# The start of a fused attention and maxout kernel: first query pair in two halves, last key piece in two loads, no later dummy matmuls, new order of the first 400 steps

## The chip, the core and the metric

One core of a Trainium2 chip runs the whole kernel. The metric is the device time of one execution in microseconds, the median of the runs shown. A profile is one execution taken by the hardware profiler; times in it count from the span's start.

## What is computed

Four batches of 12288 queries attend to 768 keys each, and the result goes through a maxout network. Keys and values are the same array: kv averaged over 4 x 4 blocks and multiplied by `w_sr`.

```python
kv_pool = kv.reshape(B, H // r, r, W // r, r, C).mean(axis=(2, 4))     # r = 4, C = 128
k = v = kv_pool.reshape(B, -1, C) @ w_sr                               # 768 x 128 per batch
a = softmax(scale * (q @ k.T)); x = (a @ v).reshape(-1, 128)           # 49152 x 128
h = max(x @ w1, x @ w2, x @ w3)                                        # 49152 x 768
out = h @ w_out
```

The weights of the network are 64-bit floats. All products are done in float16 with each operand split into a high and a low part, so that a product of two matrices is three matmuls (high by high, high by low, low by high).

## The kernel before

The 49152 queries are 96 groups of 512 (`g`); a group is four tiles of 128 (`j`). Two neighbouring groups share one load of q, a pair of 512 KB.

The work is cut into steps, each named by a short token, and the order of all steps is written out by hand in tables of tokens: `START` (the prologue and the first groups), `STEADY` (repeated 41 times) and `END`. Every engine executes its instructions in the order of the table. A token with `!` runs the step on VectorE, with `%` on GpSimd, instead of its usual engine. The tokens that matter here:

- `kv.s.i`, `wd.n.h`, `qd`: loads of a kv piece (12 of 512 KB), of half a weight matrix (8 of 384 KB) and of q. All are issued by SyncE (SP) into one queue, as are the transposing DMAs.
- `add`, `gat`, `end`: kv pieces are added in place, then transposed and summed by fp32 matmuls with the identity (gather). `gathered` copies the result out of PSUM, `gathered_peak` takes its maximum, `gathered_project` multiplies it by `w_sr`, `gathered_hi` and `gathered_lo` split it into the keys' two parts `k_hi`, `k_lo`; `value` transposes these by DMA into `v_hi`, `v_lo`.
- `qc`, `qp`, `qu`, `qh`, `ql`, `qt`, `qe`: a group of q is multiplied by a column scale, its row maximum is taken over the pair (`q_peak`; with `!` a sum of absolute values on ScalarE), a power of two is made of it, the high and the low part are formed and transposed by DMA into `qT`.
- `S`: the scores of one tile, six matmuls into `ps_s` (two buffers). `m`: their row maximum `mx` and the bias `nb` (VectorE); `e`: exponential (ScalarE); `c`: its high part `ahl` (ScalarE, or VectorE with `!`); `l`: its low part (GpSimd); `lt`: a transposing DMA into `aT`.
- `X`: attention weights by values, for group 0 tile by tile, later in two halves per group; `xh`, `xl` split the result.
- `H`: six matmuls for one 128-column slice of the hidden layer into two buffers `ps_h`; `R`, `M`: relu and maximum of the two; `C`, `L`: high and low part; `O`: three matmuls with `w_out`, six for a group's last slice.
- `wm`, `ws`, `wl`: a 64-bit weight piece becomes fp32 (ScalarE scales, VectorE shifts and adds the low bits into `w_three`); `wr` subtracts the first matrix from the others, `wh` and `wo` split into `d_hi`, `d_lo`. `dsize`, `turn_w1`, `product`, `usize` are the few matmuls of the weights' own sizing and product.
- `warm.n`: n dummy matmuls of 256 columns with the identity into `ps_o`; nothing reads them (`keep_warm`, line 349).

In the kernel before, `START` has four `warm.8` before the first `S` and 12 `warm.4` and one `warm.8` up to the first `H`, 88 dummies in all. The profile shows all instructions at line 105, the wrapper that keeps program order, so tiles identify them.

Of the kernel before, what the change touches and what calls it, by code (L numbers as in the profile page):

```python
# [9 lines left out]
F32 = mybir.dt.float32  # L10
F16 = mybir.dt.float16
# [10 lines left out]
def kernel(  # L22
# [34 lines left out]
    R = 4  # L57
# [67 lines left out]
    def times(t, src, by, by2=None):  # L125
# [261 lines left out]
    class Keys:  # L387
# [18 lines left out]
        def load(self, s, i):  # L406
            piece = kvp.tile([P, PIECE], F32, name="kv_piece")
            src = kv[self.b].rearrange("(s h i) (w r) c -> s i h w (r c)", s=KS, i=R, w=KW)
            sp_dma.dma_start(out=piece, in_=src[s, i])
            self.pieces[s, i] = piece  # L410
# [177 lines left out]
    def q_load(s):  # L588
        t = qp.tile([P, SJ, C], F32, name="q_sb", bufs=2)
        sp_dma.dma_start(out=t, in_=q_src[s])  # L590
        st["q"][s] = t
# [8 lines left out]
    def q_peak(s, summed=False):  # L600

        assert not {2 * s, 2 * s + 1} & set(todo["qc"])
        row = qp.tile([P, 1], F32, name="q_row", bufs=2)
        if summed:
            act.activation(
                out=qp.tile([P, 3 * HALF_F], F16, name="q_abs", bufs=1)[:, :SJ * C], in_=st["q"][s].rearrange("p j c -> p (j c)"),
                func=AF.Abs, accum_out=row,
            )
        else:
            dve.tensor_reduce(out=row, in_=st["q"][s], axis=AX.XY, op=ALU.max, apply_absolute_value=True)  # L610
        st["qr"][s] = row

    def q_up(s):
        row = st["qr"][s]
        up = qp.tile([P, 1], F32, name="q_up", bufs=2)
        dve.tensor_scalar(
            out=row.bitcast(I32), in0=row.bitcast(I32), scalar1=EXPO, scalar2=None, op0=ALU.bitwise_and
        )
        dve.tensor_scalar(out=up, in0=row, scalar1=TINY, scalar2=2.0 ** -14, op0=ALU.max, op1=ALU.mult)
        dve.reciprocal(out=up, in_=up)  # L620
        st["qr"][s] = (row, up)

    def q_hi(g, on=None):
        hl = qp.tile([P, NJ, 2, C], F16, name="q_hl", bufs=2)
        if on:
            on.tensor_scalar(
                out=hl[:, :, 0], in0=q_half(g), scalar1=st["qr"][g // 2][1], scalar2=None, op0=ALU.mult
            )
        else:
            act.mul(out=hl[:, :, 0], in_=q_half(g), mul=st["qr"][g // 2][1])  # L630
        st["qhl"][g] = hl

    def q_lo(g):
        t, hl = q_half(g), st["qhl"][g]
        up = st["qr"][g // 2][1]
# [12 lines left out]
    def q_exps(s):  # L648
        sc = qp.tile([P, 1], F32, name="q_sc", bufs=4)
        dve.tensor_scalar(  # L650
            out=sc, in0=st["qr"][s][0], scalar1=TINY, scalar2=KT[2 * s // GPB].g_exp, op0=ALU.max, op1=ALU.mult
# [25 lines left out]
    def soft_bias(g, j, negated):  # L677
        nb = tiny.tile([P, 1], F32, name="nb")
        dve.tensor_scalar(
            out=nb, in0=negated, scalar1=st["sc"][g // 2], scalar2=LN_A_UP, op0=ALU.mult, op1=ALU.add  # L680
# [489 lines left out]
```

## Time and profile before

| | before |
|---|---|
| median of 3 runs | 1973.16 us (1973.13 to 1973.49) |
| span of the profiled execution | 1971.1 us, 29575 instructions |
| TensorE busy | 1961.7 us (100%) |
| VectorE busy | 1473.6 us (75%) |
| ScalarE busy | 1486.3 us (75%) |
| GpSimd busy | 1271.3 us (64%) |
| DMA | 284.61 MB, mean 144 GB/s |

The profile gives no device time of the profiled execution other than its span, from the first to the last instruction; the runs' median lies 2.1 us above it. Busy shares are means over the run. Matmuls are pipelined and their ends are modelled, so a busy TensorE says that matmuls followed each other, not that they were useful: the dummies count too. Idle time of another engine costs nothing as long as TensorE has work.

### The profile page before, as it was taken

The numbers are of one execution on the slowest core, as the hardware profiler recorded it, in microseconds if no ns is written. First come the engines' busy times: TensorE is split into PE (matmuls) and PEld (weight loads), VectorE is DVE, ScalarE is ACT, GpSimd is POOL, SyncE is SP. The second block draws the span as 40 slices with busy tenths as digits, with TensorE's granted clock in tenths as the row PEclk, the third lists the DMA queues.
The fourth block names the chain that finished last, engine by engine and source line by source line (L and its number), as shares of the span: only waits on it lengthen the run. The fifth ranks groups of instructions, "written<-read, shape, count | busy, mean of one in ns | idle before, by whom it ended". The sixth has DMA issues, their size and how long they took to land.

```text
span 1971.1 us, 29575 instructions
## 1 busy us (share of the span) xinstructions
PE 1961.7 (100%) x9869; PEld 964.2 (49%) x9869; DVE 1473.6 (75%) x2558; ACT 1486.3 (75%) x2620; POOL 1271.3 (64%) x934
## 2 busy tenths in 40 slices
PE   8999999999999999999999999999999999999999
PEld 7444444444444444444444444444444444444444
DVE  7998987777767787777667777777766676767677
ACT  5866677787777777777777777777777777777775
POOL 3644566666676666766666676666676666666663
PEclk9999999999999999999999999999999999999999
DMA  9977577767678767767678767866776666756763
GB/s 285 179 166 147 111 161 138 148 132 138 129 152 162 158 145 159 147 126 137 138 133 164 156 147 157 164 128 129 137 145 136 129 126 128 144 123 127 134 128 81
DMA packets 845241, 284.61 MB, mean 144 GB/s; under 512 B 818720, under 2 KB 819872, under 8 KB 845088
## 3 DMA queue, kind: packets, MB, share of 16 engines
q1 hardware_dynamic: 844800, 282.58, 70.5%
q8 instruction: 78, 1.28, 0.3%
q14 instruction: 75, 0.61, 0.1%
q10 hardware_dynamic: 288, 0.13, 0.0%
HBM read 53.54 MB, written 25.17 MB: 40 GB/s over the span
## 4 chain that ended last, share of the span: by engine, by line
PE 98%; DMA 1%; DVE 0%; ACT 0%; SPq 0%; issue 0%; DVEq 0%; ACTq 0%
PE ps_h L105 38%; PE ps_o L105 22%; PE ps_x L105 19%; PE ps_s L105 19%; DMA kv_piece<-in_kv_dram 0%; DMA aT<-ahl 0%; SPq L105 0%; ACT a L105 0%; DVE q_row L105 0%; DVE kv_piece L105 0%; DVE k_lo L105 0%; ACT w_three L105 0%; DVE mx L105 0%; ACT ahl L105 0%; ACT k_hi L105 0%
## 5 line engine op out<-in xcount | busy, mean ns | idle before, releaser
L105 POOL TENSOR_TENSOR hl<-h,hh 128x512 f16<-128x512 f32 x461 | 551.5, 1202 | 513.8 <-ACT hh L105 512.0
L105 POOL TENSOR_TENSOR ahl<-a,ahl 128x768 f16<-128x768 f32 (+1 forms) x378 | 618.2, 1655 | 136.3 <-ACT ahl L105 103.3
L105 DVE SCALAR_TENSOR_TENSOR h<-ps_h,h 128x512 f32<-128x512 f32 x574 | 395.5, 689 | 344.5 <-PE ps_h L105 190.2
L105 ACT ACTIVATE h<-ps_h 128x512 f32<-128x512 f32 x574 | 342.3, 596 | 284.1 <-PE ps_h L105 274.0
L105 PE MATMUL ps_h<-xh,d_hi 128*128 128x512 f16 x1148 | 435.1, 379 | 0.0
L105 PE MATMUL ps_h<-xh,d_lo 128*128 128x512 f16 x1148 | 435.1, 379 | 0.0
L105 PE MATMUL ps_h<-xl,d_hi 128*128 128x512 f16 x1148 | 435.1, 379 | 0.0
L105 DVE TENSOR_REDUCE mx<-ps_s 128x1 f32<-128x768 f32 x384 | 365.1, 951 | 50.3 <-PE ps_s L105 50.2
L105 ACT ACTIVATE a<-ps_s,nb,q_sc 128x768 f32<-128x768 f32 x384 | 379.6, 989 | 14.1 <-DVE nb L105 13.4
L105 PE MATMUL ps_s<-k_hi,qT 128*128 128x384 f16 x1536 | 374.6, 326 | 0.0
L105 ACT CAST hh<-h 128x512 f16<-128x512 f32 x577 | 336.6, 613 | 42.6 <-DVE h L105 41.4
L105 PE MATMUL ps_x<-aT,v_hi 128*128 128x512 f16 (+1 forms) x1188 | 367.2, 373 | 0.2 <-DMA aT<-ahl 0.2
L105 PEld LDWEIGHTS <-d_hi 128*128 128x128 f16 x2308 | 225.8, 98 | 256.6
L105 PE MATMUL ps_o<-hh,wo 128*128 128x512 f16 x1140 | 339.1, 379 | 0.0
L105 PEld LDWEIGHTS <-qT 128*128 128x128 f16 x2304 | 225.4, 98 | 187.4
L105 ACT CAST ahl<-a 128x768 f16<-128x768 f32 x367 | 300.1, 829 | 5.3
L105 PEld LDWEIGHTS <-wo 128*128 128x128 f16 x1710 | 167.3, 98 | 191.7
L105 PE MATMUL ps_s<-k_lo,qT 128*128 128x384 f16 x768 | 250.2, 326 | 0.0
L105 PE MATMUL ps_x<-aT,v_lo 128*128 128x512 f16 (+1 forms) x594 | 220.2, 373 | 0.0
L105 PE MATMUL ps_o<-hl,wo 128*128 128x512 f16 x570 | 216.0, 379 | 0.0
L105 PEld LDWEIGHTS <-v_hi 128*128 128x128 f16 x1188 | 115.3, 98 | 134.7 <-issue 0.5
L105 PEld LDWEIGHTS <-d_lo 128*128 128x128 f16 x1154 | 112.9, 98 | 120.9
(151 smaller groups left out, 1459.1 us busy)
## 6 DMA issues: line engine op xcount, KB each, us to landing
kv_piece<-in_kv_dram SPq DMA_DIRECT2D x48, 512.0 KB, 4.5
q_sb<-in_q_dram SPq DMA_DIRECT2D x48, 512.0 KB, 4.4
out_dram<-o_sb SPq DMA_DIRECT2D x95, 256.0 KB, 2.0
aT<-ahl SPq DMA_TRANSPOSE x384, 4.0
kv_piece<-in_moe_w_dram SPq DMA_DIRECT2D x6, 384.0 KB, 9.4
qT<-q_hl SPq DMA_TRANSPOSE x96, 3.6
o_turned<-o_planes SPq DMA_TRANSPOSE x95, 3.4
kv_piece<-in_moe_w_out_dram SPq DMA_DIRECT2D x2, 384.0 KB, 7.7
```

The lines of the kernel that those rows point to most:

```text
L105: return lambda **kw: tc.keep_in_program_order(op(**kw))
```

## The change

1. The first q pair is loaded in two halves, one group each: `unit` and `unit_q` map the step numbers, so that `qd`, `qp`, `qu` and `qe` exist once for group 0, once for group 1 and then once for each pair (49 in place of 48). The first half is loaded first of all, the second behind two kv pieces.
2. The last kv piece (`kv.0.2`) is loaded in two halves of 256 KB.
3. All dummies after the first score tile are gone (12 `warm.4` and the `warm.8` after the first scores), and two batches between gather and scores. Three `warm.8` remain, one at the very start.
4. `START` has a new order up to step 399 (408 before). From there on the tables are word for word the same, and up to there both have issued the same work. In these steps some work has moved between engines: two of the kv additions (`add.1.0.1%`, `add.0.2.3.0%`) to GpSimd; two subtractions `wr` and two products `qc` from VectorE to GpSimd; seven casts `c`, four high parts `qh`, one `wh` and one `gathered` from ScalarE to VectorE; the first maximum of q partly to ScalarE.

```diff
@@ the table, two of its rows around the first H
-        "dsize.1 product dsized.1 ratio S m c X wo.1.0 l e X usize l xh warm.4 c l m usized xl produced qe S e H R",
+        "dsized.1 ka ratio lt c X m usize wo.1.0 e qt S qe usized lt xh wo.2.0 qd S xl produced c l m H R e M H R lt m",
...
-        def load(self, s, i):
-            piece = kvp.tile([P, PIECE], F32, name="kv_piece")
-            src = kv[self.b].rearrange("(s h i) (w r) c -> s i h w (r c)", s=KS, i=R, w=KW)
-            sp_dma.dma_start(out=piece, in_=src[s, i])
-            self.pieces[s, i] = piece
+        def load(self, s, i, *us):
+
+            if (s, i) not in self.pieces:
+                self.pieces[s, i] = kvp.tile([P, PIECE], F32, name="kv_piece")
+            piece = self.pieces[s, i]
+            src = kv[self.b].rearrange("(s h i) (w r) c -> s i h w (r c)", s=KS, i=R, w=KW)[s, i]
+            if us:
+                x = slice(us[0] * PIECE // KU, (us[0] + 1) * PIECE // KU)
+                piece, src = piece[:, x], src[:, :, x]
+            sp_dma.dma_start(out=piece, in_=src)
...
-    def q_load(s):
-        t = qp.tile([P, SJ, C], F32, name="q_sb", bufs=2)
-        sp_dma.dma_start(out=t, in_=q_src[s])
-        st["q"][s] = t
+    def unit(g):
+
+        return g if g < 2 else g // 2 + 1
+
+    def unit_q(u):
+        s = max(u - 1, 0)
+        js = slice(u * NJ, (u + 1) * NJ) if u < 2 else slice(0, SJ)
+        return s, js
+
+    def q_load(u):
+        s, js = unit_q(u)
+        if s not in st["q"]:
+            st["q"][s] = qp.tile([P, SJ, C], F32, name="q_sb", bufs=2)
+        sp_dma.dma_start(out=st["q"][s][:, js], in_=q_src[s][:, js])
...
-    halves_q, eights_q = (list(range(n)) for n in (NG, NG // 2))
+    halves_q, eights_q = (list(range(n)) for n in (NG, NG // 2 + 1))
```

The rest of the diff takes `unit(g)` for `g // 2` where a scale of q is read, and gives `q_row` and `q_up` three buffers for two and `q_sc` five for four.

**SP's queue, from the last kv loads to the first attention weights.** `in_moe_w_dram` and `in_moe_w_out_dram` are the network's weights. Before:

```order
L105 DMA kv_piece<-in_kv_dram 128x1x1024 x10
L105 DMA kv_piece<-in_moe_w_dram 128x768 x4
L105 DMA_TRANSPOSE qT<-q_hl 128x8x128
L105 DMA q_sb<-in_q_dram 128x1024
L105 DMA kv_piece<-in_moe_w_out_dram 128x3x256
L105 DMA kv_piece<-in_moe_w_dram 128x768 x2
L105 DMA kv_piece<-in_moe_w_out_dram 128x3x256
L105 DMA_TRANSPOSE qT<-q_hl 128x8x128
L105 DMA_TRANSPOSE v_lo<-k_lo 128x6x128
L105 DMA_TRANSPOSE v_hi<-k_hi 128x6x128
L105 DMA_TRANSPOSE aT<-ahl 128x12x128 x4
```

Now:

```order
L105 DMA kv_piece<-in_kv_dram 128x1x512 x2
L105 DMA kv_piece<-in_moe_w_dram 128x768 x3
L105 DMA_TRANSPOSE qT<-q_hl 128x8x128
L105 DMA kv_piece<-in_moe_w_dram 128x768 x2
L105 DMA q_sb<-in_q_dram 128x1024
L105 DMA_TRANSPOSE qT<-q_hl 128x8x128
L105 DMA kv_piece<-in_moe_w_out_dram 128x3x256
L105 DMA_TRANSPOSE v_hi<-k_hi 128x6x128
L105 DMA kv_piece<-in_moe_w_dram 128x768
L105 DMA kv_piece<-in_moe_w_out_dram 128x3x256
L105 DMA_TRANSPOSE v_lo<-k_lo 128x6x128
L105 DMA_TRANSPOSE aT<-ahl 128x12x128 x4
```

The first transposition stands behind three weights and no longer four; the second stands ahead of three weights; the values' two are apart, with weights between.

**VectorE, from the split of the keys to the first score maximum.** Before:

```order
L105 SCALAR_TENSOR_TENSOR k_lo<-ps_x,k_up,k_hi 128x512
L105 SCALAR_TENSOR_TENSOR k_lo<-ps_s,k_up,k_hi 128x256
L105 TENSOR_SCALAR q_sc<-q_row,g_exp 128x1
L105 TENSOR_SCALAR w_three<-w_three 128x384
L105 TENSOR_REDUCE mx<-ps_s 128x1
```

Now:

```order
L105 SCALAR_TENSOR_TENSOR k_lo<-ps_s,k_up,k_hi 128x256
L105 SCALAR_TENSOR_TENSOR k_lo<-ps_x,k_up,k_hi 128x512
L105 TENSOR_SCALAR q_sc<-q_row,g_exp 128x1
L105 TENSOR_SCALAR w_three<-w_three 128x384
L105 TENSOR_SCALAR q_sc<-q_row,g_exp 128x1
L105 TENSOR_SCALAR w_three<-w_three 128x384
L105 TENSOR_REDUCE mx<-ps_s 128x1
```

Two shifts of weights (`ws.0.1`, `ws.1.1`, the fourth and the fifth weight loaded) now stand ahead of the first maximum; before it was one.

**TensorE, at the end of the first H.** Before, a score tile followed it:

```order
L105 LDWEIGHTS d_lo
L105 MATMUL ps_h<-xh,d_lo 128x512
L105 LDWEIGHTS d_hi
L105 MATMUL ps_h<-xl,d_hi 128x512
L105 LDWEIGHTS qT
L105 MATMUL ps_s<-k_hi,qT 128x384
```

Now the next H follows at once:

```order
L105 LDWEIGHTS d_lo
L105 MATMUL ps_h<-xh,d_lo 128x512
L105 LDWEIGHTS d_hi
L105 MATMUL ps_h<-xl,d_hi 128x512
L105 LDWEIGHTS d_hi
L105 MATMUL ps_h<-xh,d_hi 128x512
```

The score tile that stood between the first two H now stands ahead of both.

## Rows read from the trace of the kernel before

**Rows 1.** The page's head and the busy time of the engines.

```profile
span 1971.1 us, 29575 instructions
...
PE 1961.7 (100%) x9869; PEld 964.2 (49%) x9869; DVE 1473.6 (75%) x2558; ACT 1486.3 (75%) x2620; POOL 1271.3 (64%) x934
```

**Rows 2.** Busy time by stretch: PE, PEld, DVE, ACT, POOL; clock, DMA share, GB/s.

```profile
27.00:48.90 21.90, 21.65 (x209) 17.39 (x207) 21.26 (x55) 20.85 (x42) 14.37 (x16) 1.00 1.07 227
48.90:97.02 48.12, 48.12 (x242) 23.55 (x241) 44.53 (x81) 43.19 (x80) 30.04 (x21) 1.00 0.91 177
97.02:1971.10 1874.08, 1870.88 (x9280) 904.34 (x9277) 1390.63 (x2388) 1415.48 (x2489) 1222.83 (x890) 1.00 0.70 140
```

**Rows 3.** TensorE's timeline: start, us, operation, count, idle before and its releaser.

```profile
4.90 1.89 PE L105 MATMUL ps_o<-ident 128*128 128x256 f16 x8
...
15.44 2.05 PE L105 MATMUL ps_h<-ident,kv_piece 128*128 128x128 f32 x16 [1.17 <-DVE kv_piece L105]
...
27.09 0.81 PE L105 MATMUL ps_s<-k_hi,qT 128*128 128x384 f16 x4
...
29.04 2.35 PE L105 MATMUL ps_o<-ident 128*128 128x256 f16 x20
...
48.90 0.38 PE L105 MATMUL ps_h<-xh,d_hi 128*128 128x512 f16 x1
```

**Rows 4.** The chain of waits in order of time: start, us, what.

```profile
23.43 0.87 PE ps_o L105 x8
...
34.21 5.24 DMA aT<-ahl
...
39.49 1.17 PE ps_x L105 x18
...
48.09 0.97 PE ps_s L105 x6
...
95.08 1.94 PE ps_o L105 x9
```

**Rows 5.** VectorE's timeline from the last kv addition to the first xl.

```profile
20.63 1.29 DVE L105 TENSOR_TENSOR kv_piece<-kv_piece 128x512 f32<-128x512 f32 x2 [0.34 <-DMA kv_piece<-in_kv_dram]
...
28.26 0.96 DVE L105 TENSOR_REDUCE mx<-ps_s 128x1 f32<-128x768 f32 x1
...
32.04 0.35 DVE L105 TENSOR_SCALAR w_three<-w_three 128x384 int32<-128x384 int32 x1
...
33.52 0.73 DVE L105 TENSOR_SCALAR w_three<-w_three 128x384 int32<-128x384 int32 x1
...
48.49 0.68 DVE L105 SCALAR_TENSOR_TENSOR xl<-ps_x,xh 128x512 f16<-128x512 f32 x1
```

**Rows 6.** GpSimd's timeline in the same stretch.

```profile
28.40 1.27 POOL L105 TENSOR_TENSOR q_sb<-q_sb,col_row 128x512 f32<-128x512 f32 x1 [0.33 <-DMA q_sb<-in_q_dram]
32.20 5.76 POOL L105 TENSOR_TENSOR ahl<-a,ahl 128x384 f16<-128x384 f32 x6 [2.53 <-DVE ahl L105]
```

**Rows 7.** ScalarE's timeline at the first weight piece.

```profile
21.56 0.56 ACT L105 ACTIVATE w_three<-kv_piece 128x384 f32<-128x384 f32 x1 [2.04 <-DMA kv_piece<-in_moe_w_dram]
```

**Rows 8.** Two stretches of 1 us around the first transposing DMA, columns as in rows 2.

```profile
24.00:25.00 1.00, 1.00 (x9) 0.96 (x8) 0.98 (x3) 0.82 (x2) 0.00 (x0) 1.00 1.45 57
25.00:26.00 1.00, 1.00 (x7) 0.77 (x6) 0.95 (x4) 0.35 (x1) 0.00 (x0) 1.00 0.23 56
```

**Rows 9.** Views of ahl, w_three, q_sb in the start: count, min/median/max ns, first and last start.

```profile
L105 DVE CAST ahl<-a x5: 548/550/799, 31.6 to 91.8; 128x768 f16<-128x768 f32 x5
...
L105 DVE TENSOR_TENSOR w_three<-w_three x2: 546/666/786, 37.6 to 39.2; 128x384 f32<-128x384 f32 x2
L105 DVE TENSOR_SCALAR d_hi<-w_three,d_up x1: 408/408/408, 51.2 to 51.2; 128x384 f16<-128x384 f32 x1
...
L105 DVE TENSOR_TENSOR q_sb<-q_sb,col_row x2: 680/850/1019, 30.5 to 59.7; 128x512 f32<-128x512 f32 x2
```

**Rows 10.** SP's queue at the first transposition of the values.

```profile
28.20 4.57 SPq L105 DMA_TRANSPOSE v_lo<-k_lo  x1
```

More of the change, by code (lines that the diff above doesn't have):

```diff
@@ L598, in q_cols, with q_peak @@
         (on or pool).tensor_tensor(out=t, in0=t, in1=col_row.unsqueeze(1).to_broadcast([P, NJ, C]), op=ALU.mult)
-    def q_peak(s, summed=False):
-        assert not {2 * s, 2 * s + 1} & set(todo["qc"])
-        row = qp.tile([P, 1], F32, name="q_row", bufs=2)
+    def q_peak(u, summed=False):
+        s, js = unit_q(u)
+        assert not [g for g in (2 * s, 2 * s + 1) if unit(g) == u and g in todo["qc"]]
+        row = qp.tile([P, 1], F32, name="q_row", bufs=3)
+        t = st["q"][s][:, js]
         if summed:
             act.activation(
-                out=qp.tile([P, 3 * HALF_F], F16, name="q_abs", bufs=1)[:, :SJ * C], in_=st["q"][s].rearrange("p j c -> p (j c)"),
+                out=qp.tile([P, 3 * HALF_F], F16, name="q_abs", bufs=1)[:, :t.shape[1] * C], in_=t.rearrange("p j c -> p (j c)"),
                 func=AF.Abs, accum_out=row,
@@ L609, in q_peak @@
         else:
-            dve.tensor_reduce(out=row, in_=st["q"][s], axis=AX.XY, op=ALU.max, apply_absolute_value=True)
-        st["qr"][s] = row
+            dve.tensor_reduce(out=row, in_=t, axis=AX.XY, op=ALU.max, apply_absolute_value=True)
+        st["qr"][u] = row
     def q_up(s):
         row = st["qr"][s]
-        up = qp.tile([P, 1], F32, name="q_up", bufs=2)
+        up = qp.tile([P, 1], F32, name="q_up", bufs=3)
         dve.tensor_scalar(
@@ L626, in q_hi @@
             on.tensor_scalar(
-                out=hl[:, :, 0], in0=q_half(g), scalar1=st["qr"][g // 2][1], scalar2=None, op0=ALU.mult
+                out=hl[:, :, 0], in0=q_half(g), scalar1=st["qr"][unit(g)][1], scalar2=None, op0=ALU.mult
             )
         else:
-            act.mul(out=hl[:, :, 0], in_=q_half(g), mul=st["qr"][g // 2][1])
+            act.mul(out=hl[:, :, 0], in_=q_half(g), mul=st["qr"][unit(g)][1])
         st["qhl"][g] = hl
@@ L634, in q_lo @@
         t, hl = q_half(g), st["qhl"][g]
-        up = st["qr"][g // 2][1]
+        up = st["qr"][unit(g)][1]
         dve.scalar_tensor_tensor(
@@ L648, in q_exps @@
     def q_exps(s):
-        sc = qp.tile([P, 1], F32, name="q_sc", bufs=4)
+        sc = qp.tile([P, 1], F32, name="q_sc", bufs=5)
         dve.tensor_scalar(
-            out=sc, in0=st["qr"][s][0], scalar1=TINY, scalar2=KT[2 * s // GPB].g_exp, op0=ALU.max, op1=ALU.mult
+            out=sc, in0=st["qr"][s][0], scalar1=TINY, scalar2=KT[2 * max(s - 1, 0) // GPB].g_exp, op0=ALU.max, op1=ALU.mult
         )
@@ L679, in soft_bias @@
         dve.tensor_scalar(
-            out=nb, in0=negated, scalar1=st["sc"][g // 2], scalar2=LN_A_UP, op0=ALU.mult, op1=ALU.add
+            out=nb, in0=negated, scalar1=st["sc"][unit(g)], scalar2=LN_A_UP, op0=ALU.mult, op1=ALU.add
         )
@@ L692, in soft_exp @@
             out=a.rearrange("p (h k) -> p h k", h=2), in_=st["ps"].pop((g, j)), func=AF.Exp,
-            bias=st["nb"].pop((g, j)), scale=st["sc"][g // 2], accum_out=sums(g)[:, j:j + 1],
+            bias=st["nb"].pop((g, j)), scale=st["sc"][unit(g)], accum_out=sums(g)[:, j:j + 1],
         )
```

58 rows, old and new, of the table START are left out of this document.

## The prediction

> **What bounds the kernel now.** I read the page first. TensorE is counted busy for 1961.7 us of a span of 1971.1 us [rows 1]; the reader is to see that only 9.4 us of the whole run are idle on it, so nothing but the matmul work itself, or what fills it without use, can be saved. The stretches say where: from 97.02 us to the end TensorE is busy 1870.88 of 1874.08 us, from 48.90 to 97.02 us all of it, from 27.00 to 48.90 us 21.65 of 21.90 us [rows 2]. But this last stretch is full only because of the dummy matmuls: one batch of 20 alone took 2.35 us, 118 ns each [rows 3]. So there is one question: how early does the stream of useful matmuls become dense, and how much of it is done by then?
>
> A common point makes that measurable. After 408 steps of the old table and 399 of the new one, both kernels have issued the same work: 21 score tiles S, 8 attention products X, 15 hidden products H, 12 projections O. What follows is word for word the same. In the kernel before TensorE ends this work at 95.08 + 1.94 = 97.02 us [rows 4]. The change of the time is the change of this point, since the 1874 us behind it are dense.
>
> The chain of waits says what sets the start: the last gathers and a dummy batch of 0.87 us at 23.43 us, then score tiles and exponentials, then a transposing DMA for the first attention weights, issued at 34.21 us and 5.24 us long, which releases the first X at 39.49 us [rows 4]. The first H follows at 48.90 us [rows 3].
>
> **The change, part by part.** *Loads.* The bytes ahead of the last kv piece are the same 13 pieces of 512 KB, in 15 loads. VectorE waited 0.34 us for the last one and added at 20.63 us [rows 5]; I leave it there. The last addition was 1.29 us for two halves in sequence; now one half is on GpSimd, at most 1.27 us for 512 columns [rows 6], and its data come half a piece (0.64 us) earlier. Both halves end near 21.3 us, 0.5 us earlier. Behind them 16 passes of the last gather take some 2.0 us [rows 3], so the gather ends near 23.2 instead of 23.43 us.
>
> *Weights and the first scores.* The first weight piece reached ScalarE at 21.56 us [rows 7], about 1 us after the last kv piece, so the third lands near 23.5. Now ScalarE converts three weights before it copies the last gathered keys; its queue holds that copy until 24.1 us, and with the projection and the high part as before the first score could start near 26.0 instead of 27.09 us [rows 3]. The transposed q agrees: its DMA is now behind three weights and not four, 1 us less. That the two dummy batches there go is in this figure.
>
> *VectorE before the first maximum.* In the new order it shifts the fourth and the fifth weight ahead of the first maximum. These load behind the transposing DMA, around which the DMA engines almost stopped: 57 and 56 GB/s between 24 and 26 us [rows 8]. Fourth at 27.0, fifth at 28.0 us, a conversion of 0.56 us [rows 7] and a shift of 0.35 us: the first maximum starts near 28.8 us, where it stood at 28.26 us [rows 5]. The 1.1 us of the start are lost in this wait.
>
> *VectorE from the first maximum to the first xl.* Before: 48.49 - 28.26 = 20.23 us, without a listed wait [rows 5]. Out go two subtractions (0.67 us each), one high part's shift (0.35) and one product with the column scale (0.7); in come two casts (0.55 each), one weight high part (0.41) and one q high part, which I estimate from the latter's 384 columns at 0.5 [rows 9]. Sum -0.4 us: xl near 48.6 us, as before.
>
> *From the first X to the first H.* Before, 48.90 - 39.49 = 9.41 us. Out go four dummies, 4 x 118 ns = 0.47 us; in comes one score tile, 0.97 us [rows 4], which was behind the first H before and so is not new work. When X starts is set by the transposing DMA. Ahead of it in SP's queue stand the same eight weights, one q load and four transposing DMAs; SP already stood 4.57 us on one of them [rows 10]. Two things change: the queue starts its first transposition 1 us earlier, and it now goes from copies to transpositions three times and not twice. One such turn costs at most 2 us by the gap of [rows 8], and part of that is the transposition itself, which is there before too. So X comes between 1.0 us earlier (the start alone) and 1.0 us later (a whole turn on top); I take 0.3 us earlier, a choice a little on the early side of the middle.
>
> *From the first H to the common point.* TensorE needs 48.12 us of dense work there [rows 2], less the moved score tile 47.15 us. Two H now follow each other without a score tile between; the second waits for the relu and maximum of the first, which I put at 0.4 us (0 to 0.7). VectorE was busy 44.53 us of this stretch [rows 2]; it gains five casts and three q high parts (2.75 + 1.5 us) and loses two column products (1.7): 47.1 us. That just fits, without slack to spare: 0, at worst +2.5 us (the rule below).
>
> *Clock and the dummies.* The later dummies cost 0.47 us where they were on the path and nothing elsewhere. If they kept the clock up, their absence has a price, below.
>
> **Sum** at the common point: -0.5 (dummies) - 0.3 (first X) + 0.4 (two H in a row) + 0 (VectorE) = -0.4 us. The span becomes 1970.7 us. The page gives the profiled execution's span alone; the median of the runs shown, 1973.16 us, lies 2.1 us above it, and I keep this distance: 1972.8 us. With both ends of the terms the sum goes from -1.5 (X 1.0 earlier, no gap) to +3.7 us (X 1.0 later, gap 0.7, VectorE 2.5), 1971.7 to 1976.9 us. A measurement of this kernel can tell about 0.2%, 3.9 us: I forecast no change that large.
>
> *A rule against the moves to GpSimd.* A shift of weights on VectorE took 0.35 us at 32.04 us and 0.73 us at 33.52 us [rows 5], when GpSimd was in its subtractions from 32.20 us on [rows 6]. The casts show it too: 0.55 us, but 0.80 at worst [rows 9]. The Trainium skill, GPSIMD Engine Reference, Specifications, says that GpSimd's SBUF interfaces are shared with VectorE, with contention for VectorE instructions that use two ports or two inputs; the two rows agree. In this change GpSimd takes two more kv additions, products and subtractions, while VectorE gets casts. If all ten added casts and high parts up to the common point met it at +0.25 us each (0.80 - 0.55), that is 2.5 us more on an engine without slack: the upper end above, and rival 2.
>
> **The rivals.**
> 1. *The start is carried through.* If the weights land before VectorE asks for them, its chain begins 1.1 us earlier (27.2 us), xl comes at 47.5 us, and the first X and H move with it. With the dummies' 0.5 that is 1.6 us, with the queue's 1.0 on top 2.6 us: 1970.6 to 1971.6 us. For it: GpSimd and ScalarE are unloaded. Against: the DMA queue was full until the first X. Its bound is VectorE, whose idle time up to the common point is 48.12 - 44.53 = 3.6 us even if nothing new went into it: 1969.6 us. Chance 0.26, and 0.04 for more than 3.9 us.
> 2. *VectorE or the DMA queue becomes the bound.* X 1.0 us later, or the casts slowed by GpSimd, or both, give +1 to +3.7 us: 1974.2 to 1976.9 us. Chance 0.16.
> 3. *The clock falls, slower.* Without dummies TensorE's useful work between 27 and 49 us is ten S (9.7 us), four X (4.0), and about 2.2 us of transposes and the weights' product: 16 of 22 us, in bursts with gaps. The rows show what a low clock costs: the first eight dummies, at 4.90 us behind an idle start, took 1.89 us, 236 ns each, against 118 ns later [rows 3]; that is the step from 1.2 to 2.4 GHz, although the granted clock in the stretches stands at 1.00. At 1.2 GHz throughout, 16 us become 32 us in place of 22: +10 us; over half of the stretch +5 us: 1978 to 1983 us. It decides if useful matmuls between 28 and 49 us show twice their spacing. For it: the dummies stand in the kernel before. Against: a gap of 1.17 us at 15.44 us [rows 3], with little around it, left the matmuls after it at full speed. The Trainium skill, TensorE: Matmul & The Clock Gate, section on PSUM-queue depth-cycling, reports just this: a kernel that cycles through PSUM banks idles briefly between groups, and its clock goes up and down. No row here shows it. Chance 0.09.
> 4. *The change does nothing beyond removing dummies* is inside the forecast: their time turns to idle time and the end stays.
>
> **How the numbers follow.** Forecast 0.45 (-1.5 to +1 us), rival 1 0.26 (and 0.04 beyond 0.2%), rival 2 0.16, rival 3 0.09. Faster by over 0.2% means a gain of 3.9 us: 0.04. Slower by over 0.2%: 0.09, rival 3 alone. Within: 0.87. The range leaves out rival 3 and the tip of rival 1, and goes from VectorE's whole idle time gained (-3.6) to the upper end of the sum (+3.7): 1969.6 to 1976.9 us.
>
> **What would show it.** Right: first score near 26 us, first maximum near 28.8 us behind a wait for a weight, X near 39 us, first H near 49.4 us behind ten scores, TensorE idle in many short gaps before it, and the common point within 1.5 us of 97.0. Wrong: the first maximum before 27.8 us and the first H before 48 us (rival 1); VectorE at over 98% with TensorE waiting for maxima after 50 us, or X after 40.5 us (rival 2); score matmuls 320 ns apart (rival 3).

## The result, and the profile after

The changed kernel takes 1988.47 us (median of 4 runs, 1987.33 to 1990.03) against 1973.33 us for the kernel before beside it: ratio 1.0076, 95% interval [1.0064, 1.0089], 15.1 us slower. The forecast was 1972.8 us. The profiled execution is 15.2 us longer too; its page:

```profile
span 1986.3 us, 29452 instructions
...
PE 1963.5 (99%) x9805; PEld 960.5 (48%) x9805; DVE 1482.7 (75%) x2570; ACT 1477.7 (74%) x2607; POOL 1280.8 (64%) x940
```

By the busy shares nothing happened to VectorE: 75% before [rows 1] and after. The stretches of the changed kernel say where to look (columns as in rows 2): gather to first maximum, then to the first `xl`, just ahead of the first H, then to 112.25 us, where the score tile behind the common point has just begun, then the rest.

```profile
24.00:29.65 5.65, 4.62 (x27) 3.12 (x27) 5.54 (x17) 3.79 (x8) 2.00 (x2) 1.00 0.94 282
29.65:54.32 24.67, 18.02 (x148) 12.98 (x146) 24.04 (x52) 18.90 (x38) 18.97 (x18) 0.91 0.93 188
54.32:112.25 57.93, 51.59 (x244) 23.89 (x243) 55.56 (x89) 36.07 (x68) 31.55 (x22) 0.98 0.77 153
112.25:1986.30 1874.05, 1869.89 (x9273) 903.72 (x9271) 1384.47 (x2387) 1414.27 (x2488) 1222.32 (x890) 1.00 0.70 139
```

The last stretch is as long as the one behind the common point was before (1874 us) and TensorE is dense in it: nearly all that is lost, is lost ahead of it. Until then VectorE is busy for 24.04 of 24.67 and 55.56 of 57.93 us, and TensorE, which was busy for nearly all of both stretches before [rows 2], idles for 13 us. TensorE's timeline of the changed kernel at the first score, the longest wait for a score buffer, the first X, the first H, the last matmul of the common work, a wait in the H behind it and the score tile behind that H:

```profile
28.01 0.81 PE L105 MATMUL ps_s<-k_hi,qT 128*128 128x384 f16 x4 [0.45 <-ACT k_hi L105]
...
37.63 0.48 PE L105 MATMUL ps_s<-k_hi,qT 128*128 128x384 f16 x2 [2.23 <-ACT a L105]
...
41.15 0.31 PE L105 MATMUL ps_x<-aT,v_hi 128*128 128x128 f16 x1
...
54.70 0.63 PE L105 MATMUL ps_h<-xh,d_hi 128*128 128x512 f16 x1
...
109.20 0.38 PE L105 MATMUL ps_o<-xl,w1o 128*128 128x512 f16 x1
...
111.44 0.38 PE L105 MATMUL ps_h<-xh,d_hi 128*128 128x512 f16 x1 [1.21 <-DVE h L105]
...
112.08 0.49 PE L105 MATMUL ps_s<-k_hi,qT 128*128 128x384 f16 x2
```

The same score tile before:

```profile
98.15 0.49 PE L105 MATMUL ps_s<-k_hi,qT 128*128 128x384 f16 x2
```

The common point is the end of the projection at 109.20 + 0.38 = 109.58 us, where it was 97.02 us: 12.6 us of the 15.2 are lost by then. The H behind it waits for VectorE, so that the next score tile comes 13.9 us later than before; the last 1.3 us are lost further on. What TensorE waited for between 24 and 125 us (total, times, longest, in us):

```profile
PE ps_s L105 <- ACT a L105: 5.9, 5, 2.2
PE ps_h L105 <- DVE h L105: 4.0, 4, 2.0
PE ps_h L105 <- DVE u_top L105: 1.5, 1, 1.5
```

Before, the same view of 24 to 100 us names a single wait of 0.2 us. The exponential `a` is ScalarE's, but ScalarE is busy for only 18.90 of 24.67 us up to the first `xl`: it waits for `nb`, which VectorE makes, as the same view of ScalarE from 24 to 112 us says:

```profile
ACT a L105 <- DVE nb L105: 11.1, 9, 2.7
```

So VectorE sets the pace. A place where it can be seen, VectorE's timeline and under it GpSimd's:

```profile
77.84 2.00 DVE L105 TENSOR_TENSOR hl<-h,hh 128x512 f16<-128x512 f32 x1
79.77 2.12 DVE L105 SCALAR_TENSOR_TENSOR q_hl<-q_sb,q_up,q_hl 128x512 f16<-128x512 f32 x1
81.81 0.68 DVE L105 SCALAR_TENSOR_TENSOR h<-ps_h,h 128x512 f32<-128x512 f32 x1
...
83.38 0.94 DVE L105 TENSOR_REDUCE mx<-ps_s 128x1 f32<-128x768 f32 x1
```

```profile
77.47 3.88 POOL L105 TENSOR_TENSOR ahl<-a,ahl 128x768 f16<-128x768 f32 x2 [2.26 <-issue]
81.31 1.60 POOL L105 TENSOR_TENSOR hl<-h,hh 128x512 f16<-128x512 f32 x1
82.87 2.09 POOL L105 TENSOR_TENSOR ahl<-a,ahl 128x768 f16<-128x768 f32 x1
```

`hl` takes 0.68 us elsewhere and 2.00 here, `q_hl` 0.74 and 2.12; each ends about half a microsecond behind the end of a GpSimd subtraction. The `h` and `mx` that follow, read from PSUM, keep their 0.68 and 0.94 us beside GpSimd work of the same kind. The Trainium skill, Trainium Architecture — The Big Picture, section What this means for kernel authors, says that VectorE and GpSimd contend for one shared port pair, and that it is "an exclusive lock (not a bandwidth split)". These rows agree: what is lost is the remainder of a GpSimd instruction, not a share of one's own time.

### The profile page after: what moved, and what is told of

It is laid out like the page before. It is cut to its first block, busy times and chain, and to the rows that moved or that the text cites. A ratio compares the mean times of both kernels' runs of the same rounds, so it can differ in the third digit from the quotient of the medians.

```text
span 1986.3 us, 29452 instructions
## 1 busy us (share of the span) xinstructions
PE 1963.5 (99%) x9805; PEld 960.5 (48%) x9805; DVE 1482.7 (75%) x2570; ACT 1477.7 (74%) x2607; POOL 1280.8 (64%) x940
## 3 DMA queue, kind: packets, MB, share of 16 engines
q8 instruction: 77, 1.26, 0.3%
## 4 chain that ended last, share of the span: by engine, by line
PE 94%; DVE 3%; DMA 1%; issue 1%; SPq 0%; ACT 0%; POOL 0%; DVEq 0%; ACTq 0%; POOLq 0%
PE ps_h L105 37%; PE ps_o L105 21%; PE ps_x L105 18%; PE ps_s L105 18%; DMA kv_piece<-in_kv_dram 1%; DVE mx L105 1%; DVE h L105 0%; DVE ahl L105 0%; DVE q_hl L105 0%; DVE w_three L105 0%; DMA o_turned<-o_planes 0%; SPq L105 0%; DVE hl L105 0%; DVE w_e L105 0%; DVE nb L105 0%
## 5 line engine op out<-in xcount | busy, mean ns | idle before, releaser
L105 ACT CAST hh<-h 128x512 f16<-128x512 f32 x577 | 336.3, 613 | 41.5 <-DVE h L105 40.5
L105 ACT CAST ahl<-a 128x768 f16<-128x768 f32 x360 | 294.4, 829 | 5.4
```

The costliest lines, as they stand in the source:

```text
L105: return lambda **kw: tc.keep_in_program_order(op(**kw))
```

## The measure used for the experiments

From the first score maximum to the fourth `xl` VectorE does nearly the same work in all kernels, and both ends are rows of its timeline. The kernel before, to the first `xl` and from there to the fourth:

```profile
28.26:48.49 20.23, 19.98 (x197) 16.38 (x196) 19.59 (x52) 19.66 (x38) 13.12 (x13) 1.00 1.07 216
48.49:106.93 58.44, 58.44 (x294) 28.56 (x293) 54.19 (x94) 50.00 (x92) 35.08 (x25) 1.00 0.96 183
sum 78.67, PE 78.42 PEld 44.94 DVE 73.78 ACT 69.66 POOL 48.19; mean PE 39.21 PEld 22.47 DVE 36.89 ACT 34.83 POOL 24.10
```

The changed kernel:

```profile
29.65:54.32 24.67, 18.02 (x148) 12.98 (x146) 24.04 (x52) 18.90 (x38) 18.97 (x18) 0.91 0.93 188
54.32:120.59 66.27, 59.93 (x285) 27.98 (x284) 63.13 (x101) 41.56 (x77) 35.02 (x25) 0.98 0.76 153
sum 90.94, PE 77.95 PEld 40.96 DVE 87.17 ACT 60.46 POOL 53.99; mean PE 38.97 PEld 20.48 DVE 43.58 ACT 30.23 POOL 26.99
```

The whole is 12.3 us longer; VectorE is 13.4 us longer busy. Its groups by shape in the two spans tell new work from stretched work (count, busy us, mean ns). Before:

```profile
L105 DVE SCALAR_TENSOR_TENSOR h<-ps_h,h 128x512 f32<-128x512 f32 x17 | 11.6, 685 | 2.8 <-ACT h L105 1.6 <-PE ps_h L105 1.1
...
L105 DVE SCALAR_TENSOR_TENSOR q_hl<-q_sb,q_up,q_hl 128x512 f16<-128x512 f32 x6 | 4.7, 783 | 0.0
...
L105 DVE CAST ahl<-a 128x768 f16<-128x768 f32 x5 | 3.0, 600 | 0.0
L105 DVE SCALAR_TENSOR_TENSOR d_lo<-w_three,d_up,d_hi 128x384 f16<-128x384 f32 x4 | 2.5, 630 | 0.0
```

Changed:

```profile
L105 DVE SCALAR_TENSOR_TENSOR h<-ps_h,h 128x512 f32<-128x512 f32 x17 | 11.6, 683 | 1.7 <-PE ps_h L105 1.6
L105 DVE CAST ahl<-a 128x768 f16<-128x768 f32 x12 | 8.9, 751 | 0.0
L105 DVE SCALAR_TENSOR_TENSOR q_hl<-q_sb,q_up,q_hl 128x512 f16<-128x512 f32 x6 | 6.3, 1053 | 0.0
...
L105 DVE SCALAR_TENSOR_TENSOR d_lo<-w_three,d_up,d_hi 128x384 f16<-128x384 f32 x4 | 3.9, 982 | 0.0
L105 DVE TENSOR_SCALAR q_hl<-q_sb,q_up 128x512 f16<-128x512 f32 x4 | 3.3, 835 | 0.0
```

Added work, priced at an unstretched duration: seven casts at 0.55 us (3.9), four q high parts at 0.48 (1.9), a maximum of q that the new order does on VectorE (1.2) and a weight's high part (0.4), less three products with the column scale at 0.67 (2.0), two subtractions at 0.55 (1.1) and a shift (0.35): 3.9 us. The other 9.5 us of the 13.4 are operations made longer. That is a sum over rows, not yet a cause; the runs below test it.

One word for what follows: *excess* is the time of VectorE's operations above the shortest with the same tiles and shape in any of the runs, added up over its timeline from 24 us to the common point. Before it is 5.6 us, in the changed kernel 16.1; the expectations below are written with 5.4 and 16.4. In the changed kernel the 46 operations that read PSUM have 0.4 us of it together, the 51 on one or two columns 0.1 us. Of the 54 others, which read SBUF alone, 27 run while a GpSimd instruction runs and have 15.3 us; the 27 that meet none have 0.2 us. Before, 20 of 46 met one and had 4.8 us, the other 26 had 0.2 us. So the excess lies beside GpSimd's work in both kernels, at 0.24 us an operation before and 0.57 us in the change.

## The experiments

Theory 1: VectorE's operations that read SBUF are stretched beside GpSimd's work, and the new table puts more of them there. Theory 2: without dummies the clock falls. Theory 3: VectorE simply has too much work. Theory 4: the split loads start everything later.

| kernel | median, us | ratio to before, 95% | first max at | to first xl | to fourth xl |
|---|---|---|---|---|---|
| before | 1973.3 | | 28.26 | 20.23 | 58.44 |
| changed | 1988.5 | 1.0064 to 1.0089 | 29.65 | 24.67 | 66.27 |
| split loads in old order | 1974.4 | 0.9994 to 1.0012 | 29.28 | 20.21 | 58.11 |
| before, no later dummies | 1975.2 | 0.9999 to 1.0017 | 28.98 | 20.94 | 58.73 |
| changed, dummies back | 1987.7 | 1.0059 to 1.0084 | 30.50 | 24.34 | 67.46 |
| changed, 11 operations back on ScalarE | 1982.2 | 1.0030 to 1.0055 | 30.46 | 23.74 | 60.95 |
| new order, old engines | 1987.4 | 1.0060 to 1.0087 | 30.55 | 26.13 | 64.09 |
| old order, new engines | 1987.2 | 1.0058 to 1.0083 | 28.78 | 26.96 | 65.26 |
| changed, GpSimd fills for subtractions | 1981.0 | 1.0026 to 1.0051 | 29.16 | 23.11 | 60.39 |
| before, the same fills | 1973.3 | 0.9992 to 1.0009 | 28.70 | 20.09 | 58.11 |
| new start, old rest | 1977.0 | 1.0010 to 1.0027 | 30.34 | 21.09 | 58.38 |
| old start, new rest | 1991.3 | 1.0076 to 1.0103 | 32.68 | 24.35 | 67.25 |
| 11 back, and fills | 1979.9 | 1.0020 to 1.0045 | 30.67 | 20.78 | 60.86 |
| 11 back, dummies back | 1981.1 | 1.0024 to 1.0053 | 29.48 | 24.17 | 60.97 |
| 11 back, fills, dummies back | 1978.6 | 1.0016 to 1.0035 | 30.59 | 23.04 | 59.65 |

The last three columns are from one profiled execution each; the last two count from the first maximum to the first `xl` and from there to the fourth. The first maximum moves by 0.7 us between kernels that share the old start (28.26, 28.70 and 28.98 us) and by 1.5 us between those that share the new one (29.16 to 30.67 us), so small differences there mean nothing.

**The parts alone.** The loads split, in the old order of steps:

```diff
-        kv.0.2 ... kv.0.3 ... qd qp qu qe
+        kv.0.3 ... kv.0.2.0 kv.0.2.1 ... qd qd qp qp qu qu qe qe
```

> The split of the first q pair and of the last kv piece put into the old order of steps, with the old dummies. Before is 1973.3 us, the change 1988.5. Theory 1 (contention: in the new order VectorE's operations with two inputs or two ports lie beside GpSimd's work and are stretched, some 11 us in all): the old order keeps the old neighbours, so 1972 to 1976 us, and VectorE's excess over its shortest operations stays near the 5 us of before. Theory 2 (clock: the missing dummies let TensorE fall to half speed): the dummies are here, so also 1972 to 1976 us, granted clock 1.00. Theory 3 (VectorE simply has more work in the new order): the same. Theory 4 (the loads: q in two halves and the last piece in two start the whole chain later): the first maximum comes 1 to 1.4 us later than 28.3 us and the time is 1974 to 1977 us.

+0.65 us, not told apart from none and inside every theory's range. The first maximum came 1.0 us later, as theory 4 said, but behind it nothing moved. Theory 4 falls as the main cause of 15 us. The dummies alone, out of the kernel before:

```diff
-  ... S warm.8 m e warm.4 wm.3.0 warm.4 m warm.4 S ...
+  ... S m e wm.3.0 m S ...
```

> The kernel before, its order and loads, without the 13 batches of dummies behind the first score tile. Nothing else is left out. Theory 2 (clock): TensorE idles between scores, its clock falls, and the time goes up by 2 to 5 us, 1975 to 1978 us; score matmuls show twice their spacing somewhere between 28 and 49 us. Theories 1, 3 and 4: 1972 to 1974 us, since the work on VectorE, which sets the pace there, is that of before.

+1.5 us, with an interval that reaches zero. 1975.2 us lies above the range of theories 1, 3 and 4 and at the lower edge of theory 2's, but theory 2's sign is missing: every 5 us stretch from 25 to 115 us shows a granted clock of 1.00. TensorE idled nearly half of 30 to 40 us and did not slow down, so the time is not the clock's.

**The clock in the changed kernel.** It does fall there: 0.68 between 40 and 45 us, behind waits of 2.23 and 0.73 us, 0.84 and 0.82 between 50 and 60 us. That is a part-time fall from 2.4 to 1.2 GHz: an H matmul started every 0.43 us at 54.70 us and every 0.215 us at 57 us. The dummies put back:

```diff
-  ... S S wl.0.1 c ...          usize ...
+  ... warm.8 S warm.4 S ...     warm.12 usize ...
```

> The changed kernel with 44 dummies put back into TensorE's gaps (8, 4, 16 and 4 ahead of the third to sixth score tile, 12 ahead of the usize matmul). Theory 2 (clock): the two stretches at half clock (39.5 to 43.1 and 53.1 to 56.8 us) go, at most 1.8 us each, 1984.5 to 1987 us; if the clock were the main cause, 1975 to 1980 us. Theories 1 and 3: VectorE is the bound there, so the matmuls get faster and then wait: 1987 to 1990 us.

-0.8 us, with overlapping intervals and inside the range of theories 1 and 3. The two stretches at half clock are gone, but a new one came in the same execution: 0.90 between 80 and 85 us, 0.76 between 85 and 90 us, behind a wait of 2.01 us for VectorE's `h`. So this run lifts the clock early on and not throughout. In the two kernels further down in which VectorE is relieved the same dummies gave -1.1 and -1.3 us with the clock at 1.00. These are net of the time that the dummies themselves take, which no run separates. So the clock is worth about 1 us net; its falls stand behind the waits.

**Work back to ScalarE.** Seven of the casts and the four q high parts, where they stand:

```diff
-  ... l c! ws.2.1 c S m lt wm.3.0 l qh! l e ...
+  ... l c ws.2.1 c S m lt wm.3.0 l qh l e ...
```

> The changed kernel with 7 of its casts c and 4 of its q high parts moved back from VectorE to ScalarE, at the places where they stand. Theory 1 (contention): VectorE loses 11 operations of 0.55 to 2.1 us, 7 us at their shortest and some 10 us as stretched; what stays is stretched as before, and ScalarE takes 7 to 8 us more: 1978 to 1983 us, VectorE's excess still 10 us or more. Theory 3 (amount of work alone): 1974 to 1981 us, with the excess down as the casts go. Theory 2 (clock): 1986 to 1990 us.

1982.2 us, inside the range of theory 1, with 14.4 us of excess left, as it said; theory 3's range ends 1.2 us lower. VectorE's busy time in the measure falls from 87.2 to 80.8 us, the time from 90.94 to 84.69: 6.4 and 6.3 us. VectorE is the bound, one for one. The ranges overlap too far for this to tell theories 1 and 3 apart.

**Order or engines?** The two other corners. In each some forty tokens change their engine; one of the first corner's is shown:

```diff
-  ... wl.1.1 turn_w1.1 wh.2.0! S e ...
+  ... wl.1.1 turn_w1.1 wh.2.0 S e ...
```

> The changed kernel's order, loads and missing dummies, but each step of the first 399 on the engine that it had before (the n-th cast where the n-th cast was, and so on). If the cost lies in what moved between engines (more on VectorE, which then waits beside GpSimd): 1974 to 1978 us, VectorE's excess over its shortest operations 5 to 9 us. If it lies in the order itself: 1982 to 1988 us. From the run with eleven casts back (1982.2 us, excess still 15 us) theory 1 expects the middle: the two q products and two subtractions leave GpSimd too, so 1976 to 1982 us.

> The other corner: the old order with the split loads and the old dummies (1974.4 us), each step of the first 399 on the engine that it has in the change. If the cost lies in what moved between engines: 1982 to 1988 us, VectorE's excess over 12 us and its share between 50 and 95 us over 97%. If it lies in the order: 1974 to 1977 us. Theory 1 (the stretching hits what runs on VectorE from SBUF beside GpSimd, in either order): 1979 to 1984 us.

Each alone costs nearly as much as both together, 14 of 15 us. Theory 1's ranges, 1976 to 1982 and 1979 to 1984 us, both missed: it expected a split, and the effects don't add. The old order with the new engines shows what theory 1 describes (excess 15.6 us, VectorE 86.77 of 92.22 us busy). In the new order with the old engines VectorE is busy for 80.09 of 90.22 us, with 11.6 us of excess, and another thing is seen, a queue. ScalarE's timeline, and TensorE's behind it:

```profile
32.74 0.19 ACT L105 ACTIVATION_READ_ACCUMULATOR a<-ps_s,nb,q_sc 128x1 f32 x1
36.47 0.61 ACT L105 ACTIVATE d_hi<-w_three,d_up 128x384 f16<-128x384 f32 x1 [3.54 <-DVE d_up L105]
36.99 0.97 ACT L105 ACTIVATE a<-ps_s,nb,q_sc 128x768 f32<-128x768 f32 x1
```

```profile
38.11 0.80 PE L105 MATMUL ps_s<-k_hi,qT 128*128 128x384 f16 x2 [3.99 <-ACT a L105]
```

With `wh.2.0` back on ScalarE at its new place, the second exponential stands behind a step that waits 3.54 us for VectorE. That is 4 of the 14 us; no run takes the other 10 apart. Order and engines can't be priced one by one here: the loss with either is nearly the loss with both.

**GpSimd's subtractions taken away.** This tells theory 1 from theory 3: VectorE keeps every operation, in the same order.

```diff
         for k in range(0, NK, n):
             sl = slice(k, k + n)
-            (on or pool).tensor_tensor(out=ahl[:, 1, sl], in0=a[:, sl], in1=ahl[:, 0, sl], op=ALU.subtract)
+            if on or g > 5:
+                (on or pool).tensor_tensor(out=ahl[:, 1, sl], in0=a[:, sl], in1=ahl[:, 0, sl], op=ALU.subtract)
+            else:
+                tc.keep_in_program_order(nc.gpsimd.memset(ahl[:, 1, sl], 0.0))
```

`hidden_lo` likewise for g up to 3.

> The changed kernel, with GpSimd's subtractions for the low parts l (groups 0 to 5) and L (groups 0 to 3) replaced by fills with zero, also on GpSimd; these low parts are left out of the computation. VectorE keeps every operation and the order. Theory 1 (VectorE's operations are stretched while GpSimd reads and writes): VectorE's excess between 24 us and the common point falls from 16.4 to 4 to 8 us and the time to 1976 to 1981 us. Theory 3 (VectorE has too much work of its own): excess or not, 1986 to 1989 us. If fills stretch VectorE as much as subtractions, the excess falls only as GpSimd's busy time does.

> The same replacement in the kernel before, as the control: the low parts of groups 0 to 5 and hidden low parts of groups 0 to 3 on GpSimd are fills with zero, left out of the computation. Theory 1: the excess falls from 5.4 to 1 to 3 us, and the time by at most 1 to 2 us, since TensorE was already dense: 1971 to 1973.5 us. Theory 3 and all others: no change, 1972.5 to 1974.5 us.

1981.0 us, 7.5 us faster (the upper end of what theory 1 expected; theory 3's 1986 to 1989 us is out), with excess 8.5 us in place of 16.1, 7.6 less but above the 4 to 8 us that theory 1 expected. The fills also free GpSimd, 27.94 us busy in the measure for 53.99. That this alone gained the time is a rival. But VectorE's busy time in the measure falls by 7.8 us (87.17 to 79.38) and the measure by 7.4 (90.94 to 83.50), and the changed kernel's lists of waits from 24 us to the common point name GpSimd neither for TensorE nor for VectorE or ScalarE, nor the transposing DMA of the attention weights that follows its subtractions. In the kernel before, the same edit cut the excess from 5.6 to 2.6 us and gained nothing: there the stretching is hidden under a dense TensorE. VectorE's groups in the changed kernel with fills, over the same measure:

```profile
L105 DVE CAST ahl<-a 128x768 f16<-128x768 f32 x12 | 11.9, 1001 | 0.0
...
L105 DVE SCALAR_TENSOR_TENSOR q_hl<-q_sb,q_up,q_hl 128x512 f16<-128x512 f32 x6 | 4.4, 742 | 0.0
...
L105 DVE SCALAR_TENSOR_TENSOR d_lo<-w_three,d_up,d_hi 128x384 f16<-128x384 f32 x4 | 2.4, 609 | 0.0
...
L105 DVE TENSOR_SCALAR q_hl<-q_sb,q_up 128x512 f16<-128x512 f32 x4 | 1.9, 476 | 0.0
```

Means of 1053, 982 and 835 ns are 742, 609 and 476, the first two below those of before (783 and 630). Of these groups only the casts got worse, 751 to 1001 ns: some of them now run beside the fills.

**Which stretch of the order?** The new steps up to the first maximum with what is left of the old order behind it, and the reverse:

```diff
   ... wd.3.0 qe value.0 ws.0.1 qe qc ws.1.1 wd.2.1
-  m turned_w1.0 wd.3.1 S e dsize.0 S S wl.0.1 c ...
+  turned_w1.0 S m e warm.4 wm.3.0 warm.4 m warm.4 S wm.2.1 e qc! ...
```

> The changed kernel's steps up to its first score maximum (28 to 30 us), and behind it what is left of the old order, with the old engines and the old dummies. If the later start is passed on: first maximum near 29.7 us as in the change, 1974 to 1976 us, the excess of VectorE behind it near the 5 us of before. If the start alone mattered (the loads and weights land differently and upset what follows): 1978 us or more. If the start is absorbed: 1973 to 1974 us.

> The opposite: the old steps up to the first score maximum, and behind it what is left of the new order with the new engines and without dummies. If the cost lies behind the first maximum (theory 1 and the amount of VectorE's work): first maximum near 28.3 us, 1984 to 1988 us, excess 13 us or more. If it lies in the start: 1973 to 1976 us.

The new start alone costs 3.6 us (interval 2.0 to 5.3), between two of the expected ranges: 2.1 us to the first maximum in the profiled execution, 0.9 us behind it, excess 6.2 us. The rest behind the old start is slower than the change itself and than expected. Part of that is a new fault of the joint: the first maximum came at 32.68 us, behind a wait of 3.50 us for a weight. From there to the fourth `xl` it took 91.6 us, as the change does (90.9), and the excess is 15.5 us. So the larger part sits behind the first maximum.

**Both remedies.** The eleven operations back and the fills:

> Both remedies in the changed kernel: 7 casts and 4 q high parts back on ScalarE, and GpSimd's subtractions l (groups 0 to 5) and L (groups 0 to 3) as fills with zero, whose low parts are left out of the computation. Alone they gave -6.3 and -7.5 us. If they are two halves of one cause that add up: 1974 to 1977 us. If each frees VectorE until something else is the bound (the start, the clock, the order): 1977 to 1981 us.

1979.9 us: they do not add up. VectorE is now busy for 72.93 of 81.64 us, so it is no longer the bound throughout. Whether the clock took its place:

> The changed kernel with 7 casts and 4 q high parts back on ScalarE (alone 1982.2 us) and the 44 dummies put back into TensorE's gaps before the first X. If the clock becomes a cost of its own once VectorE is relieved (granted clock 0.83 between 30 and 40 us there): 1979 to 1981 us. If VectorE still sets the pace: 1981.5 to 1983.5 us.

> The same dummies in the kernel with casts back and with fills for GpSimd's subtractions (their low parts left out of the computation; alone 1979.9 us, granted clock 0.50 between 35 and 40 us). If the clock is what is left of the loss next to the start (3.6 us by the run with the new start alone): 1976 to 1978 us, granted clock 1.00. If the clock costs nothing even here: 1979 to 1981 us, and what is left lies in the order on VectorE and ScalarE between 28 and 60 us.

1981.1 and 1978.6 us with clocks of 1.00: about 1 us each, with overlapping intervals, and both medians between the two ranges that were to decide. In the kernel with both remedies 3.0 us are left in the measure, of which 2.4 lie behind the first `xl`. One row could account for them, VectorE's at 55.16 us, with GpSimd's fills beside it and TensorE's wait behind it:

```profile
55.16 3.32 DVE L105 CAST ahl<-a 128x768 f16<-128x768 f32 x1
58.41 0.67 DVE L105 SCALAR_TENSOR_TENSOR h<-ps_h,h 128x512 f32<-128x512 f32 x1
```

```profile
55.06 0.73 POOL L754 MEMSET ahl<- 128x768 f16 x1
55.73 0.98 POOL L846 MEMSET hl<- 128x512 f16 x2
56.66 1.41 POOL L754 MEMSET ahl<- 128x768 f16 x2
```

```profile
59.14 0.38 PE L105 MATMUL ps_h<-xh,d_hi 128*128 128x512 f16 x1 [2.52 <-DVE h L105]
```

A cast of 0.55 us did not end until five fills in a row had ended at 58.07 us. No run was made with this last contention alone removed, so that it is the whole of the remainder is argued from the row, not shown. No kernel that was tried beats the one before.

## Why the prediction was wrong

**What bounds the kernel** was read rightly in the main: the start decides. The common point moved by 12.6 us, in three parts: 1.4 us to the first maximum, 4.4 us from there to the first `xl`, 6.7 us from there on. But the time did not change by this alone. The H right behind the common point lost 1.4 us more to VectorE, and 1.3 us followed further on.

**Loads and the last addition, -0.5 us:** wrong. The last gather ended at 24.67 us, not 23.2. GpSimd's half of the last addition took 1.27 us as predicted (21.29 to 22.56 us), but VectorE's half, beside it, took 1.18 us at 21.93 us, where two halves in a row took 1.29 [rows 5]. Shared between the two engines the addition won next to nothing, and the last data came later: this half waited for its DMA until 21.93 us, where the last addition before began at 20.63 us [rows 5].

**First score 26.0, first maximum 28.8 us:** measured 28.01 and 29.65, and with no wait for a weight: VectorE was busy. ScalarE reached its first weight at 22.82 us, not 21.56 [rows 7]. By the run with the new start alone, start and loads together cost 3.6 us; the sum had nothing for them.

**VectorE from first maximum to first xl, -0.4 us:** measured +4.4 us. The operations were counted right. Their durations were taken from the quiet rows of the kernel before [rows 9]; here two additions of a weight's low bits (`wl`) took 1.17 and 1.26 us, where the shortest took 0.55, and a high part of q with its low part 0.89 and 1.24.

**VectorE behind the first H, "0, at worst +2.5 us":** this is the step that failed, and with the term above it most of the loss. Measured are +6.7 us up to the common point and 1.4 us in the H behind it. The price of 0.25 us for an operation beside GpSimd is the mean of the kernel before (0.24 us), and it was put on ten operations that came in. Only seven more lie beside GpSimd in the change (27 for 20), but the new order gave new neighbours to the old ones too, and the mean over all 27 is 0.57 us, up to 1.4 us at worst. So the price did not carry over to the new order, and it should have been asked of every operation that reads SBUF, not of the new ones. The sum also left out a maximum of q, 1.2 us. The added work, 3.9 us by the sum above, would have fitted into the 4.9 us that VectorE had idle in the measure (78.67 - 73.78); with the stretching it did not, and 7.5 us came back when the subtractions went.

**Rival 1** (the start carried through) did not come: the first maximum stands at 29.65 us, not before 27.8.

**Rival 2** named the mechanism (VectorE the bound, slowed by GpSimd), its chance 0.16, and sized it at +1 to +3.7 us instead of +15. Its sign of success, VectorE over 98% busy with TensorE waiting after 50 us, was nearly met: 97% up to the first `xl`, 96% behind it, with the waits of the list above. Its other sign, X after 40.5 us, was met at 41.15 us.

**Rival 3** (the clock): the doubled spacing is there, in two places, and costs about 1 us by the runs with dummies. The sign that should have decided for it was present while the mechanism was not the main cause: with the dummies back TensorE waited for VectorE instead.

**First X:** 41.15 us for 39, behind score tiles that waited 2.23 and 0.73 us for exponentials; the X itself waited for nothing. The first H came behind ten scores as predicted, at 54.70 us instead of 49.4.

## What to carry to other kernels

In these traces a VectorE operation that reads SBUF alone has no fixed duration while GpSimd runs: price a new order by which of these lie beside GpSimd instructions, and do not take the price from the old order. The rows suggest to put operations that read PSUM there, whose durations held; no run tried it. VectorE was busy for 94% of the measure before (73.78 of 78.67 us): with so little left, a contention that is invisible in the run's mean share became time. A hand-made order and its assignment of engines are one object; changing either alone here cost nearly as much as changing both.

## What the runs showed that was not expected

- Contention hits operations with one SBUF input too: a cast of 0.55 us took up to 3.32 us, and a scaling of q of 0.48 us took 1.49 us at 60.11 us in the changed kernel. What holds an operation depends, in these rows, on what GpSimd does. In the changed kernel with fills, two shifts `w_e` took 1.89 us together at 43.21 us, beside fills from 42.41 to 44.63 us, where the pair took 0.61 in the changed kernel; but `q_hl` with its two inputs, at 42.55 us beside the same fills, kept its 0.74 us, and beside subtractions it took up to 2.12. The Trainium skill, GPSIMD Engine Reference, Specifications, names VectorE instructions with two SBUF inputs or in a two-port mode; the rows of `q_hl` agree for subtractions, and whether the cast and the shift run in such a mode no row shows.
- TensorE at half use from 30 to 40 us kept a granted clock of 1.00 in the kernel before without dummies, while waits of 2.23 and 0.73 us were followed by 0.68 in the changed kernel. What makes the difference stays open.
